# One kernel, one written order against another: retention attention and a gated channel mix on one core

## The chip, the cores and the metric

The kernel runs on one core of one Trainium2 chip. The time is device microseconds (us) from the core's first to its last instruction as the run reports it; three runs of the kernel before took 430.01, 433.79 and 429.88 us, median 430.01 us. Engines are called as the profile calls them: PE multiplies matrices, PEld is its weight load, DVE is the vector engine, ACT the scalar engine, POOL the GpSimd engine, SP issues the loads. Each engine works through its own instructions in the order in which they are written and stops at an instruction whose wait is not met.

## The reference

The inputs are q, k, v of shape (4, 8, 768, 64) (batch, heads, positions, head size), a decay `lam` per head, and for the second part `mu_k`, `mu_r` (512), `w_k` (512 x 1024), `w_v` (1024 x 512), `w_r` (512 x 512), all float32.

```python
# retention, per block of 64 positions
intra = ((qb @ kb.T) * Dmask) @ vb
inter = (qb * lam_pow) @ kv_state
out[block] = intra + inter
kv_state = lam_block * kv_state + (kb * rev_pow).T @ vb
# channel mix on x = the heads side by side, 512 wide
xk = mu_k * x + (1 - mu_k) * x_prev
xr = mu_r * x + (1 - mu_r) * x_prev
k = maximum(xk @ w_k, 0)
return sigmoid(xr @ w_r) * ((k * k) @ w_v)
```

`x_prev` is x moved by one position; `Dmask[i, j]` is `lam ** (i - j)` for i >= j and zero otherwise.

## The kernel before

The 768 positions are cut into six stages of 128 positions (n = 0 to 5), a stage of all four batches at once, 512 columns. The eight heads are four pairs (hp = 0 to 3). The whole program is one list of steps, the string `ORDER`; a step is a letter and two digits, and it is written out in the order of that string. So `ORDER` sets the order of each engine's instructions and of the loads on SP's queue. Every recorded instruction has line 30 of the file, so the trace is read by tile names.

The steps of a stage n and pair hp, with the tiles that the trace shows:

- `L`, `N`: SP loads of keys (`in<-kk`, 512 KB) and of queries and values (`in<-qv`, two of 256 KB); in stage 0 one load `L` (`in<-qvk`, 1 MB). Two buffers, `in0` and `in1`, are used by turns (hp % 2). `M`: POOL clears two blocks of the buffer (`MEMSET in`), which waits for the last reader of what lay there, the step `B` of the pair that used the buffer before.
- `A`: PE, scores into `sc`. `a`: DVE, times the decay table into `mv`. `q`: DVE, decayed queries into `mv`. `k`: ACT, decayed keys.
- `U`: PE, sums into `u` (one buffer). `u`: ACT copies the state into `in`, DVE updates the state `st`, ACT copies again. `w`: a second DVE update of `st`, which frees `u`.
- `B`: PE, values into `xp` (one buffer), from `in` and `mv`.
- `e`/`E`: ACT scales `xp` into `ts`, POOL copies one column (`ts<-lastw`, `lastw<-ts`). `f`/`F`: DVE mixes; in stage 0 the result is the fp32 tile `x`. `y`/`x`: ACT and DVE split the mix into a high part `xh` and a low part `xl` (`e`, `f`, `y` serve the input of k, `E`, `F`, `x` that of r).
- `R`/`Q`: PE, one pair's part of the receptance product, for batches 0-1 and 2-3, into four `rp` banks. `s`: ACT, sigmoid into `rt`.
- `K` (f = 0 to 7): PE, one eighth of the product with `w_k`, into a `kp` bank. `h`: ACT and DVE square it into `kf`. `p`: ACT and DVE split two eighths into `k` high and low; its DVE part writes `k<-kf,k`.
- `V` (i = 0 to 7): PE, batch i // 2, half i % 2 of the product with `w_v`, into a `vp` bank. `o`: DVE multiplies by `rt`, ACT issues the output transfer. For the last batch of the last stage V56 and V57 hold the multiplication and the transfer themselves, and `o53` does nothing.

`rp`, `kp` and `vp` share four PSUM banks. Products are taken in three fp32r passes (high by high, high by low, low by high), except in stage 0, where `R` and `K` run once in fp32, with the plain weights.

The weights arrive as 8-byte numbers and are turned into fp32 on the chip: `S` loads a slice (`wst`), `c` takes the magnitude on ACT and its maximum on POOL (on DVE for the first two slices of w_r; tile `wu`, one buffer), `C` puts the bits together in three DVE instructions (`wu`, `wst`, and `wr`, `wk` or again `wst`), `D` splits the slice on ACT and DVE into high and low (`hiv`, `lov` for w_v). `T` builds the decay tables on PE, `Z` runs matrix products of zeros.

Of the kernel before, what the change touches and what calls it, by code (L numbers as in the profile page):

```python
# [480 lines left out]


ORDER = """
Sr0 cr0 Cr0 Z10 T0 L00 Sr1 Z1 A00 k00 U00 a00 Z2 B00 cr1 L01 u00 Cr1 Sr2 k01 A01 a01 E00 U01 cr2 L02 u01 e00 T1 B01
Sr3 E01 L03 T2 F00 k02 Cr2 A02 f00 R00 e01 cr3 a02 U02 B02 M10 k03 u02 F01 f01 A03 Cr3 U03 Sk0 e02 R01 E02 a03 ck0 N10
L10 L11 Q00 f02 F02 R02 u03 Sk1 k10 q10 B03 N11 M11 Ck0 U10 E03 A10 Sk2 F03 Q01 R03 Q02 L12 e03 f03 ck1 u10 a10 B10
Sk3 N12 w10 Sv0 Sv1 M12 k11 U11 A11 s00 Ck1 Q03 s01 q11 E10 e10 ck2 k12 f10 u11 s02 K00 h00 a11 F10 A12 B11 M13 w11
L13 E11 Ck2 e11 a12 ck3 U12 K01 u12 f11 N13 K02 k13 s03 F11 Ck3 K03 w12 x10 cv0 A13 q12 B12 h01 h02 p00 h03 E12 N20
Sv2 Cv0 cv1 a13 L20 Dv0 U13 K04 u13 K05 Cv1 q13 K06 h04 p01 Dv1 K07 Sv3 M20 cv2 w13 A20 k20 U20 V00 h05 y10 L21 Cv2
k21 F12 e12 f12 V02 B13 h06 cv3 Dv2 M21 u20 Cv3 p02 N21 w20 h07 Dv3 p03 y11 x11 Dr0 V04 V06 q20 Dr1 U21 A21 V01 E13  # L490
V03 e13 V05 V07 o00 o01 a20 F13 f13 Dk0 B20 o02 o03 L22 y13 x12 R10 Q10 R11 Q11 R12 Q12 N22 u21 a21 x13 y12 Dk1 R13
Q13 L23 s10 q22 K10 s11 M22 E20 q21 K11 e20 s12 s13 w21 f20 F20 k22 U22 h10 A22 x20 Dk2 B21 K12 M23 a22 Dk3 K13 K14
h11 e21 N23 E21 F21 K15 h12 K16 p10 f21 h13 k23 u22 w22 B22 h14 U23 x21 A23 K17 p11 h15 E22 F22 u23 w23 V10 h16 y20
L30 p12 V12 a23 k30 V14 y21 e22 f22 M30 q23 h17 x22 L31 N30 A30 U30 p13 k31 B23 L32 V16 E23 V11 e23 a30 F23 u30 q30
N31 w30 V13 f23 M31 U31 y22 o10 B30 e30 u31 o11 A31 y23 k32 V15 o12 V17 R20 o13 E30 N32 q32 f30 x23 Q20 R21 Q21 R22
Q22 R23 L33 k33 Q23 q31 a31 M32 s20 w31 F30 s21 x30 B31 E31 e31 U32 F31 u32 w32 A32 a32 f31 M33 K20 s22 h20 L40 N33
K21 s23 B32 E32 F32 A33 x32 U33 h21 K22 u33 N40 q33 h22 L41 K23 h23 p20 k41 p21 K24 K25 h24 K26 K27 a33 h25 V20 k40
h26 p22 h27 y30 p23 w33 e32 f32 x31 V22 y31 V21 M40 B33 U40 A40 L42 M41 q40 e33 E33 f33 V24 u40 F33 N41 a40 w40 y32
V23 y33 B40 A41 o20 E40 U41 a41 F40 u41 V26 e40 L43 V25 V27 q41 x33 k42 o21 w41 o22 M42 f40 N42 A42 o23 B41 N43 U42
M43 L50 E41 a42 k43 u42 R30 F41 q42 w42 Q30 R31 Q31 R32 Q32 e41 R33 f41 Q33 x40 B42 s30 s31 U43 x41 A43 a43 E42 F42  # L500
q43 s32 s33 u43 w43 K30 N50 q50 x42 h30 K31 K32 h31 p30 K33 K34 h32 h33 p31 K35 h34 K36 h35 K37 L51 V30 h36 y40 e42
k50 y41 V32 V34 f42 h37 p33 p32 U50 B43 E43 A50 u50 V31 V33 y42 e43 N51 k51 F43 o30 f43 a50 q51 V35 V36 A51 U51 o31
B50 e50 a51 f50 o32 V37 E50 o33 u51 R40 Q40 F50 R41 Q41 B51 R42 Q42 x50 L52 k52 L53 x43 E51 F51 R43 y43 Q43 s40 N52
U52 N53 u52 q52 A53 s41 a53 s42 A52 K40 h40 q53 K41 h41 a52 s43 k53 K42 K43 h42 p40 K44 K45 K46 h43 h44 x51 p41 h45
e51 h46 f51 p42 K47 B52 h47 U53 y50 u53 p43 y51 V40 V42 e52 V41 E52 f52 V43 V44 F52 o40 y52 V46 V45 V47 B53 o41 o42
o43 x52 e53 f53 y53 R50 Q50 R51 Q51 R52 Q52 E53 F53 x53 R53 Q53 s50 s51 K50 K51 s52 h50 s53 h51 K52 h52 K53 h53 p51
p50 K54 h54 K55 h55 K56 K57 h56 h57 p53 V50 V52 V54 p52 V51 V53 o50 o51 V56 V55 V57 o52 o53
"""


# [51 lines left out]
```

## Time and profile before

| | |
|---|---|
| runs | 429.88, 430.01, 433.79 us, median 430.01 |
| profiled execution | span 430.3 us (no other time of it is given) |
| busy: PE, PEld | 419.5 us (98%), 328.9 us (76%) |
| busy: DVE, ACT, POOL | 264.0 us (61%), 204.9 us (48%), 71.0 us (16%) |
| chain that ended last | PE 81%, DVE 7%, DMA 6%, ACT 2%, POOL 1%, issue 1% |
| read from HBM, written | 35.83 MB, 6.29 MB |

A line of the timeline has the start, the duration, the engine, the operation with output and inputs, the count, and in brackets the idle time before it with what ended that. PE is busy in 98% of the span; the stretches in which it stands are read from its timeline.

### The profile page before, as it was taken

The page shows a single profiled execution, that of the slowest core. Times are in us where ns is not written, and L with a number is a line of the kernel's source. Part 1 is how long each engine was busy: PE and PEld are TensorE (multiplying, and loading weights), DVE is VectorE, ACT ScalarE, POOL GpSimd, SP SyncE. Part 2 cuts the span into 40 slices and gives each one's busy share as a digit, 9 for nine tenths or more (in the row PEclk, how much of TensorE's full clock was granted, in tenths as well). Part 3 has the DMA queues.
Part 4 walks back from the last instruction along what each step waited for, and adds up shares of the span by engine and source line. Part 5 has one row for each costly group of instructions (what it writes and reads, how often), then busy time and mean ns, then how long its engine had stood idle before and what let it go on. Part 6 is the DMA issues. An engine that isn't in the chain of part 4 may idle for free.

```text
span 430.3 us, 7314 instructions
## 1 busy us (share of the span) xinstructions
PE 419.5 (98%) x2935; PEld 328.9 (76%) x2935; DVE 264.0 (61%) x402; ACT 204.9 (48%) x357; POOL 71.0 (16%) x142
## 2 busy tenths in 40 slices
PE   7998899999999999999999999999999999999996
PEld 4665545668888888888888888888878888888885
DVE  5886999979867674746667646555437561414411
ACT  3645686586677643344644434454244460224300
POOL 4366554331102011110020200000000000000000
PEclk9999999999999999999999999999999999999999
DMA  7889918131403213515004523004520001100001
GB/s 295 304 308 330 300 48 277 66 97 50 146 3 99 87 46 107 153 58 140 0 2 131 187 78 99 0 0 123 161 62 0 2 1 50 50 2 0 0 30 69
DMA packets 12306, 42.60 MB, mean 99 GB/s; under 512 B 1776, under 2 KB 2160, under 8 KB 10736
## 3 DMA queue, kind: packets, MB, share of 16 engines
q1 hardware_dynamic: 8672, 35.84, 26.5%
q10 hardware_dynamic: 3600, 6.29, 4.0%
q8 instruction: 23, 0.38, 0.4%
q14 instruction: 11, 0.09, 0.1%
HBM read 35.83 MB, written 6.29 MB: 98 GB/s over the span
## 4 chain that ended last, share of the span: by engine, by line
PE 81%; DVE 7%; DMA 6%; ACT 2%; POOL 1%; issue 1%; SPq 0%; DVEq 0%; ACTq 0%
PE vp L30 29%; PE kp L30 26%; PE rp L30 13%; PE xp L30 5%; PE sc L30 4%; DMA wst<-w_k 4%; PE u L30 3%; DMA in<-qv 2%; DVE wst L30 2%; DVE mv L30 1%; DVE lov L30 1%; PE table L30 1%; ACT wu L30 1%; DVE wu L30 1%; POOL wu L30 1%
## 5 line engine op out<-in xcount | busy, mean ns | idle before, releaser
L30 PE MATMUL vp<-hiv,k 128*128 128x512 f32 (+1 forms) x400 | 122.8, 384 | 1.0 <-ACT kf L30 1.0
L30 PEld LDWEIGHTS vp<-hiv,k 128*128 128x128 f32 x400 | 74.1, 188 | 16.9 <-ACT kf L30 1.4
L30 PE MATMUL vp<-lov,k 128*128 128x512 f32 (+1 forms) x200 | 76.2, 381 | 0.0
L30 PE MATMUL kp<-xh,hik 128*128 128x512 f32 x160 | 62.9, 393 | 0.0
L30 PE MATMUL kp<-xl,hik 128*128 128x512 f32 x160 | 62.3, 389 | 0.0
L30 PE MATMUL kp<-xh,lok 128*128 128x512 f32 x160 | 62.3, 389 | 0.0
L30 ACT ACTIVATE ts<-xp,omu 128x512 f32<-128x512 f32 x48 | 31.8, 684 | 62.5 <-PE xp L30 44.2
L30 DVE TENSOR_TENSOR kf<-kp,kf 128x512 f32<-128x512 f32 x40 | 27.4, 688 | 37.2 <-ACT kf L30 37.1
L30 ACT ACTIVATE kf<-kp 128x512 f32<-128x512 f32 x48 | 28.4, 594 | 37.6 <-PE kp L30 37.2
L30 ACT COPY in<-st 64x256 f32<-64x256 f32 x80 | 32.3, 404 | 22.1 <-DVE st L30 17.8
L30 PEld LDWEIGHTS vp<-lov,k 128*128 128x128 f32 x200 | 37.6, 188 | 6.9
L30 DVE TENSOR_TENSOR mv<-sc,Dt 64x512 f32<-64x512 f32 (+1 forms) x48 | 32.6, 686 | 12.3 <-PE sc L30 11.9
L30 DVE TENSOR_TENSOR xl<-ts,xh 128x512 fp32r<-128x512 f32 x40 | 27.7, 703 | 19.3 <-ACT xh L30 19.2
L30 DVE SCALAR_TENSOR_TENSOR ts<-xp,smalls,ts 128x512 f32<-128x512 f32 x40 | 29.6, 747 | 15.8 <-ACT ts L30 15.6
L30 DVE TENSOR_TENSOR mv<-in,LP 64x256 f32<-64x256 f32 x80 | 34.5, 431 | 3.2 <-DMA in<-qv 1.6
L30 DVE TENSOR_TENSOR k<-kf,k 128x1024 fp32r<-128x1024 f32 x24 | 29.1, 1223 | 10.7 <-ACT k L30 10.7
L30 DVE TENSOR_TENSOR rt<-vp,rt 128x512 f32<-128x512 f32 (+1 forms) x25 | 16.4, 665 | 31.5 <-PE vp L30 31.2
L30 PEld LDWEIGHTS kp<-xh,hik 128*128 128x128 f32 x160 | 30.0, 188 | 7.0 <-issue 0.9
L30 PEld LDWEIGHTS kp<-xh,lok 128*128 128x128 f32 x160 | 30.0, 188 | 6.3
L30 PEld LDWEIGHTS kp<-xl,hik 128*128 128x128 f32 x160 | 30.0, 188 | 6.0
L30 ACT CAST xh<-ts 128x512 fp32r<-128x512 f32 x40 | 24.1, 616 | 21.7 <-DVE rt L30 18.2
L30 DVE SCALAR_TENSOR_TENSOR st<-st,LC,u 128x256 f32<-128x256 f32 x36 | 17.2, 478 | 24.8 <-ACT in L30 20.0
(70 smaller groups left out, 586.3 us busy)
## 6 DMA issues: line engine op xcount, KB each, us to landing
in<-qv SPq DMA_DIRECT2D x40, 256.0 KB, 4.5
in<-kk SPq DMA_DIRECT2D x20, 512.0 KB, 4.6
out<-rt ACTq DMA_DIRECT2D x23, 256.0 KB, 2.0
in<-qvk SPq DMA_DIRECT2D x4, 1024.0 KB, 6.3
wst<-w_k SPq DMA_DIRECT2D x4, 1024.0 KB, 9.2
wst<-w_v SPq DMA_DIRECT2D x4, 1024.0 KB, 9.7
wst<-w_r SPq DMA_DIRECT2D x4, 512.0 KB, 7.1
out<-rt ACTq DMA_DIRECT2D x2, 128.0 KB, 1.7
```

The costliest lines, as they stand in the source:

```text
L30: return lambda *args, **kw: self.tc.keep_in_program_order(op(*args, **kw))
```

## The change

`ORDER` is written anew: the same steps, in another order, and four more. Every step of the string before is there once, and `M50`, `M51`, `M52` and `M53`, which the string before did not have, clear the buffers ahead of stage 5 as well: eight more `MEMSET` of 64 x 512 on POOL. Every `M` now stands right behind the `B` that last reads the buffer. No line outside the string changes.

```diff
 ORDER = """
-Sr0 cr0 Cr0 Z10 T0 L00 Sr1 Z1 A00 k00 U00 a00 Z2 B00 cr1 L01 u00 Cr1 Sr2 k01 A01 a01 E00 U01 cr2 L02 u01 e00 T1 B01
-Sr3 E01 L03 T2 F00 k02 Cr2 A02 f00 R00 e01 cr3 a02 U02 B02 M10 k03 u02 F01 f01 A03 Cr3 U03 Sk0 e02 R01 E02 a03 ck0 N10
-L10 L11 Q00 f02 F02 R02 u03 Sk1 k10 q10 B03 N11 M11 Ck0 U10 E03 A10 Sk2 F03 Q01 R03 Q02 L12 e03 f03 ck1 u10 a10 B10
...
+Sr0 L00 cr0 Z10 T0 Z1 A00 Sr1 k00 T2 L01 U00 Cr0 a00 Z2 B00 cr1 Sr2 A01 E00 u00 Cr1 a01 e00 L02 k01 F00 cr2 T1 U01 B01
+f00 E01 u01 F01 k02 R00 A02 Sr3 e01 R01 U02 L03 Cr2 cr3 a02 B02 M10 Sk0 N10 k03 f01 e02 E02 u02 Cr3 L10 F02 Sk1 A03
+Q00 R02 a03 f02 q10 ck0 k10 Q01 U03 B03 M11 u03 E03 e03 Ck0 L11 N11 U10 F03 f03 o53 ck1 Sk2 A10 u10 a10 Sk3 Q02 Q03
+w10 R03 B10 M12 k11 Ck1 s00 q11 U11 s01 ck2 N12 e10 E10 u11 A11 L13 Ck2 f10 L12 s03 K02 s02 ck3 k13 K00 a11 k12 K01
+F10 w11 Ck3 q12 Sv0 h00 Sv1 Sv3 U12 h02 x10 B11 M13 cv0 A12 e11 a12 h01 Cv0 K03 E11 p00 F11 h03 cv1 K04 u12 K05 Sv2
+f11 Cv1 L20 K06 B12 M20 k20 w12 Dv0 N13 cv2 Dv1 U13 Cv2 h04 A13 h05 p01 p02 L21 cv3 K07 k21 V04 y10 x11 Cv3 h06 E12
...
```

Three places at which the instructions stand otherwise now. The first is PE at the end of the opening, where the first product with w_k begins. Before, B10 (`xp_474`), U11, A11 and the last receptance part are followed by K00 (`kp_558`, four rows) and then by A12 (`sc_569`):

```order
L30 MATMUL xp_474<-mv_405,in0_104 64x64 x16
L30 MATMUL u_504<-in1_105 64x128 x8
L30 MATMUL sc_513<-in1_105 64x128 x8
L30 MATMUL rp_392<-wr1_296,x32_7_95 128x512
L30 MATMUL rp_394<-wr1_296,x32_7_95 128x512
L30 MATMUL kp_558<-x32_0_88,wk0_425 128x512
L30 MATMUL kp_558<-x32_1_89,wk0_425 128x512
L30 MATMUL kp_558<-x32_2_90,wk1_526 128x512
L30 MATMUL kp_558<-x32_3_91,wk1_526 128x512
L30 MATMUL sc_569<-in0_104 64x128 x8
L30 MATMUL xp_578<-mv_532,in1_105 64x64 x16
L30 MATMUL u_617<-in0_104 64x128 x8
```

Now, from B10 (`xp_478`) on:

```order
L30 MATMUL xp_478<-mv_389,in0_104 64x64 x16
L30 MATMUL u_510<-in1_105 64x128 x8
L30 MATMUL sc_539<-in1_105 64x128 x8
L30 MATMUL kp_557<-x32_0_88,wk0_432 128x512
L30 MATMUL kp_557<-x32_1_89,wk0_432 128x512
L30 MATMUL kp_557<-x32_2_90,wk1_501 128x512
L30 MATMUL kp_557<-x32_3_91,wk1_501 128x512
L30 MATMUL kp_569<-x32_0_88,wk0_432 128x512
L30 MATMUL kp_569<-x32_1_89,wk0_432 128x512
L30 MATMUL kp_569<-x32_2_90,wk1_501 128x512
L30 MATMUL kp_569<-x32_3_91,wk1_501 128x512
L30 MATMUL kp_578<-x32_0_88,wk0_432 128x512
```

The receptance part has gone ahead of B10, three products with w_k (K02, K00, K01) stand in a row, and U12, B11 and A12 follow only behind the third.

The second place is the conversion of w_v, on POOL and on DVE. POOL before, from the maximum of the last w_k slice (`wu_614`) over those of the four w_v slices (`wu_662`, `wu_716`, `wu_780`, `wu_867`):

```order
L30 TENSOR_SCALAR wu_614<-wu_614 128x1024
L30 TENSOR_SCALAR wu_662<-wu_662 128x1024
L30 COPY ts_705<-lastw_113 128x4
L30 COPY lastw_113<-ts_705 128x4
L30 TENSOR_SCALAR wu_716<-wu_716 128x1024
L30 MEMSET in0_104 64x512 x2
L30 TENSOR_SCALAR wu_780<-wu_780 128x1024
L30 COPY ts_829<-lastw_113 128x4
L30 COPY lastw_113<-ts_829 128x4
L30 TENSOR_SCALAR wu_867<-wu_867 128x1024
```

POOL now, the same maxima being `wu_564` and `wu_637`, `wu_675`, `wu_732`, `wu_771`:

```order
L30 TENSOR_SCALAR wu_564<-wu_564 128x1024
L30 MEMSET in1_105 64x512 x2
L30 TENSOR_SCALAR wu_637<-wu_637 128x1024
L30 COPY ts_649<-lastw_113 128x4
L30 COPY lastw_113<-ts_649 128x4
L30 COPY ts_665<-lastw_113 128x4
L30 COPY lastw_113<-ts_665 128x4
L30 TENSOR_SCALAR wu_675<-wu_675 128x1024
L30 MEMSET in0_104 64x512 x2
L30 TENSOR_SCALAR wu_732<-wu_732 128x1024
L30 TENSOR_SCALAR wu_771<-wu_771 128x1024
```

A clear (`in1`, step M13) has come ahead of the first of the four. The clear of `in0` (M20) stands ahead of the third in both, but the step whose end it waits for, B12, has moved on PE from behind K03 to behind K06. DVE before, around the bits of the second slice (`wu_716`, `wst_498`) and the low part of `k` for eighths 2 and 3 (`k2_1_765`):

```order
L30 TENSOR_SCALAR wu_716<-wu_716 128x1024
L30 SCALAR_TENSOR_TENSOR wst_498<-wst_498,wu_716 128x1024
L30 SCALAR_TENSOR_TENSOR wst_498<-wst_498 128x1024
L30 TENSOR_TENSOR mv_719<-in1_105,LP_111 64x4x64 x4
L30 TENSOR_TENSOR k2_1_765<-kf_697,k2_1_765 128x2x512
L30 TENSOR_TENSOR lov1_85<-wst_498,hiv1_768 128x1024
```

DVE now, the low part of `k` being `k2_1_764` and the bits of the third slice `wu_732`, `wst_693`:

```order
L30 TENSOR_TENSOR lov0_84<-wst_594,hiv0_727 128x1024
L30 TENSOR_TENSOR lov1_85<-wst_599,hiv1_735 128x1024
L30 TENSOR_SCALAR wu_732<-wu_732 128x1024
L30 SCALAR_TENSOR_TENSOR wst_693<-wst_693,wu_732 128x1024
L30 SCALAR_TENSOR_TENSOR wst_693<-wst_693 128x1024
L30 TENSOR_TENSOR k2_1_764<-kf_612,k2_1_764 128x2x512
L30 TENSOR_TENSOR k2_2_767<-kf_750,k2_2_767 128x2x512
```

The low part of `k` stood behind the bits of the second slice and now stands behind those of the third.

The third place is the end of DVE's program. Before, the last stage's outputs are multiplied in the order o50, o51, V56, V57, o52:

```order
L30 TENSOR_TENSOR rt_3335<-vp_3473,rt_3335 128x512
L30 TENSOR_TENSOR rt_3337<-vp_3486,rt_3337 128x512
L30 TENSOR_TENSOR rt_3370<-vp_3542,rt_3370 128x256
L30 TENSOR_TENSOR rt_3370<-vp_3581,rt_3370 128x256
L30 TENSOR_TENSOR rt_3365<-vp_3499,rt_3365 128x512
```

Now o50, V56, o51, o52, V57:

```order
L30 TENSOR_TENSOR rt_3337<-vp_3476,rt_3337 128x512
L30 TENSOR_TENSOR rt_3378<-vp_3560,rt_3378 128x256
L30 TENSOR_TENSOR rt_3360<-vp_3521,rt_3360 128x512
L30 TENSOR_TENSOR rt_3358<-vp_3494,rt_3358 128x512
L30 TENSOR_TENSOR rt_3378<-vp_3591,rt_3378 128x256
```

The multiplication of PE's very last product, which had one more behind it, is now the last itself.

More of the change, by code (lines that the diff above doesn't have):

```diff
@@ L483 @@
 ORDER = """
-Sr0 cr0 Cr0 Z10 T0 L00 Sr1 Z1 A00 k00 U00 a00 Z2 B00 cr1 L01 u00 Cr1 Sr2 k01 A01 a01 E00 U01 cr2 L02 u01 e00 T1 B01
-Sr3 E01 L03 T2 F00 k02 Cr2 A02 f00 R00 e01 cr3 a02 U02 B02 M10 k03 u02 F01 f01 A03 Cr3 U03 Sk0 e02 R01 E02 a03 ck0 N10
-L10 L11 Q00 f02 F02 R02 u03 Sk1 k10 q10 B03 N11 M11 Ck0 U10 E03 A10 Sk2 F03 Q01 R03 Q02 L12 e03 f03 ck1 u10 a10 B10
-Sk3 N12 w10 Sv0 Sv1 M12 k11 U11 A11 s00 Ck1 Q03 s01 q11 E10 e10 ck2 k12 f10 u11 s02 K00 h00 a11 F10 A12 B11 M13 w11
-L13 E11 Ck2 e11 a12 ck3 U12 K01 u12 f11 N13 K02 k13 s03 F11 Ck3 K03 w12 x10 cv0 A13 q12 B12 h01 h02 p00 h03 E12 N20
@@ L489 @@
[L489 to L507, printed above, removed]
+Sr0 L00 cr0 Z10 T0 Z1 A00 Sr1 k00 T2 L01 U00 Cr0 a00 Z2 B00 cr1 Sr2 A01 E00 u00 Cr1 a01 e00 L02 k01 F00 cr2 T1 U01 B01
@@ new lines @@
+N20 Dv2 h07 V06 e12 Dv3 p03 Dk0 V00 f12 V02 a13 V05 V07 u13 V03 F12 V01 w13 Dr0 o02 U20 q13 B13 M21 Dr1 o03 o01 E13
+A20 o00 R10 R11 F13 Q10 y11 x12 x13 Q11 R12 L22 u20 Q12 R13 e13 q20 w20 N21 Dk1 a20 Q13 f13 s10 y12 A21 U21 s11 B20
+M22 y13 u21 e20 K10 K12 q21 s12 a21 E20 s13 K11 F20 h10 Dk2 k22 K13 f20 w21 Dk3 h12 N22 B21 M23 h11 q22 E21 U22 h13
+A22 e21 K16 p10 K15 f21 L30 K17 F21 L23 K14 k30 p11 h16 u22 a22 V16 h14 h17 B22 M30 N23 w22 A23 h15 k23 y20 U23 V12
+V10 L31 y21 x20 p13 a23 E22 N30 e22 V14 p12 u23 w23 V13 k31 A30 q23 f22 F22 q30 B23 M31 x22 x21 U30 u30 L32 a30 e23
@@ new lines @@
+f23 N31 V17 E23 V11 F23 V15 y22 o13 w30 o11 R20 B30 M32 o10 A31 o12 U31 E30 R21 R22 x23 N32 y23 e30 K20 k32 u31 R23
+K22 q31 F30 w31 f30 h20 U32 a31 A32 q32 s21 B31 M33 s20 Q20 x30 e31 Q21 h22 L40 Q22 K21 Q23 N33 E31 a32 K23 f31 k40
+u32 s22 L33 K24 k33 h21 s23 F31 w32 K25 p20 A33 U33 B32 M40 h23 K26 h24 a33 u33 q33 h25 L41 p21 K27 y30 k41 h26 E32
+V24 N40 x31 V22 V20 h27 V26 A40 p23 e32 q40 F32 y31 w33 f32 p22 x32 B33 M41 E33 U40 V27 e33 u40 V25 V23 N41 f33 w40
+a40 q41 y32 y33 F33 o22 U41 A41 x33 B40 M42 o21 V21 e40 R30 R31 f40 E40 R32 u41 o20 o23 L42 L43 R33 F40 K31 K30 s30
@@ new lines @@
+K32 h30 N42 s31 k42 a41 k43 w41 K33 h31 A42 q42 h32 B41 M43 p30 U42 E41 L50 F41 K34 h33 K35 h34 Q30 Q31 a42 e41 N43
+Q32 K36 Q33 u42 h35 x40 p32 K37 p31 f41 w42 U43 q43 h36 B42 M50 s32 y40 A43 a43 E42 h37 F42 e42 N50 s33 k50 y41 p33
+V34 f42 u43 y42 V32 V36 V30 A50 w43 B43 M51 L51 U50 k51 V33 e43 q50 u50 N51 V35 V31 x42 x41 E43 a50 o32 F43 o31 V37
+R40 o30 f43 y43 R41 B50 M52 o33 x43 U51 q51 A51 R42 N52 a51 E50 L52 e50 R43 f50 K40 K42 F50 L53 u51 k52 h40 B51 M53
+k53 s40 e51 A52 s41 U52 K41 K46 h41 N53 h42 p40 q52 Q40 Q41 K47 Q42 Q43 h46 E51 q53 u52 x50 s42 f51 s43 a52 K43 K45
@@ L508 @@
+A53 U53 h47 F51 h43 B52 u53 K44 p41 y50 h44 E52 V40 e52 h45 a53 F52 V42 V46 p42 p43 V47 f52 o43 y51 V41 x51 V44 B53
+E53 V43 o40 V45 F53 e53 x52 f53 o41 R50 o42 x53 R51 R52 R53 Q50 y53 Q51 y52 Q52 s50 Q53 K53 s52 s51 K52 h52 s53 K56
+h53 h56 K57 K50 p51 h57 p53 K51 h50 K54 h51 K55 p50 V50 h54 h55 V54 p52 V55 V52 V51 o50 V53 V56 o51 o52 V57
 """
```

## The prediction

> **What bounds the kernel now.** I read the page first, then PE's timeline, then the chain of waits, then the timelines of POOL and DVE at the places that the new order touches, and the landing times of single loads. The page:
>
> ```profile
> span 430.3 us, 7314 instructions
> PE 419.5 (98%) x2935; PEld 328.9 (76%) x2935; DVE 264.0 (61%) x402; ACT 204.9 (48%) x357; POOL 71.0 (16%) x142
> PEclk9999999999999999999999999999999999999999
> ```
>
> PE is busy for 419.5 of 430.3 us, at full clock in every slice. A new order removes no product, so all that it can win or lose is PE's standing time, 10.8 us. PE's timeline says where that lies (the bracket is the idle time before the row):
>
> ```profile
> 17.26 1.13 PE L30 MATMUL table<-lone 128*128 128x512 f32 x2
> 18.90 1.16 PE L30 MATMUL sc<-in 64*128 64x128 f32 x16 [0.51 <-DMA in<-qvk]
> 39.99 1.41 PE L30 MATMUL xp<-mv,in 128*64 128x64 f32 x32 [1.35 <-DVE mv L30]
> 45.12 3.60 PE L30 MATMUL kp<-x,wk 128*128 128x512 f32 x8
> 50.30 1.09 PE L30 MATMUL sc<-in 128*64 128x128 f32 x16 [1.59 <-DMA in<-qv]
> 64.55 1.10 PE L30 MATMUL xp<-mv,in 128*64 128x64 f32 x32
> 93.04 0.50 PE L30 MATMUL vp<-hiv,k 128*128 128x512 f32 x1 [0.99 <-ACT kf L30]
> ```
>
> The chain of waits has PE's end and what follows it:
>
> ```profile
> 404.17 22.10 PE vp L30 x120
> 426.30 0.42 DVE rt L30
> 426.72 0.60 DVEq L558
> ```
>
> From 93.04 us on PE never stands until 426.27. So the new order can win at four waits ahead of that: 0.51 (A02), 1.35 (B10), 1.59 (A12) and 0.99 us (V06). B10 hides a little more: it takes 1.41 us where B12 takes 1.10, so its second half waited 0.31. Together 4.75 us. Behind them lies the tail of 430.3 - 426.3 = 4.0 us. What PE stands before 17 us is counted at nothing: its start is the same decay tables and the same first products in both orders.
>
> **The change part by part.** *A02.* PE was free at 17.26 + 1.13 = 18.39 and waited for L02, which SP issues when B00 ends. The new order puts T2 (1.13) ahead of B00, which sends the load off so much later, but puts R00 ahead of A02:
>
> ```profile
> 19.99 1.98 PE L30 MATMUL rp<-wr,x 128*128 128x512 f32 x4
> 22.42 1.04 PE L30 MATMUL xp<-mv,in 128*64 128x128 f32 x16
> 23.39 1.16 PE L30 MATMUL sc<-in 64*128 64x128 f32 x16
> ```
>
> A part R of stage 0 takes 1.8 (5.42 us for three, below), so PE comes to A02 at 18.4 + 1.8 = 20.2 and the load is in at 18.9 + 1.1 = 20.0. The 0.51 goes, with 0.2 to spare.
>
> *R02.* Here a wait comes in. Its x needs B02, then ACT's scaling, and two column copies on POOL; POOL has M10 ahead of them, which starts when B02 ends:
>
> ```profile
> 23.59 1.95 POOL L30 MEMSET in<- 64x1024 f32 x2 [1.07 <-issue]
> 25.85 0.19 POOL L30 COPY ts<-lastw 128x4 f32<-128x4 f32 x1
> 33.82 0.75 DVE L30 SCALAR_TENSOR_TENSOR x<-xp,smalls,ts 128x512 f32<-128x512 f32 x1
> 33.22 5.42 PE L30 MATMUL rp<-wr,x 128*128 128x512 f32 x12
> ```
>
> From the clear's start to the end of the second copy: 25.85 + 0.19 - 23.59 = 2.45; with DVE's 0.75 and some hand-overs 3.4. Before, A03, U03, R01 and Q00 lay between B02 and R02; now only A03 and Q00, 1.1 + 1.8 = 2.9. New wait 0.5.
>
> *B10.* ACT stood for the second w_k slice, with U10's copies queued behind, and DVE stood behind those:
>
> ```profile
> 36.73 1.15 ACT L30 ACTIVATE wu<-wst 128x1024 f32<-128x1024 f32 x1 [1.44 <-DMA wst<-w_k]
> 27.38 9.33 DMA wst<-w_k
> ```
>
> In the new order SP issues Sk1 ahead of L11 and N11, right behind L10, and R03 (1.8) goes ahead of B10 together with Q02 and Q03, while R01 and U10 leave the stretch before it for an earlier place. I put the issue at 24 to 26 us; with 9.3 for the landing the slice is in at 33.5 to 35.6 instead of 36.7, and what follows on ACT and DVE comes 1.1 to 3.2 earlier. PE comes to B10 later: it was free at 39.99 - 1.35 = 38.64, and has now 0.51 less (A02), 0.5 more (R02) and Q03's 1.8 more ahead of it, 40.4. The 1.35 and the 0.31 both go. B10, U11 and A11 (1.0 each) then end at 43.4, where K02 starts.
>
> *A12.* The 1.59 is the load N12, which B10's end releases; it takes
>
> ```profile
> 41.43 8.73 DMA in<-qv
> 66.46 14.00 PE L30 MATMUL kp<-x,wk 128*128 128x512 f32 x32
> ```
>
> 8.7 us, and PE had only 50.30 - 1.59 - 41.43 = 7.3 of work in that time. Eight products of kp make one K00 to K07, so a K takes 14.00 / 4 = 3.5. Three of them now stand ahead of U12, B11 and A12, 10.5 us in place of one: the load is in about 5 us before PE asks. The 1.59 goes.
>
> *U12.* What comes next on PE behind those three needs k12 (ACT, on the load L12) and w11 (DVE, behind the conversion Ck2). U12 falls at 43.4 + 10.5 = 53.9. DVE's list to w11 ends at 52.4 to 53.4, if I lay its steps behind one another. L12 needs A11's end, 43.4; with the 8.7 of the load above it lands at 52.1, and k12's two scalings (about 0.9) end at 53.0. Both are less than 1.0 ahead of PE, so I take 0.3 (0 to 1.0).
>
> *V06.* Its 0.99 was the squaring h07 on ACT, which empties the bank that V06 writes and stood behind ACT's parts of the w_v conversion. In the new order V04 and V06 take banks that are emptied early, and h06 and h07 free those of V00 and V02; h07 ends by the list some 3.5 us behind the wait of V04 (next part), and the product on its bank starts some 7 us behind it. The 0.99 goes.
>
> *V04.* This is the largest new wait. POOL now has M20, which waits for B12, ahead of the maximum of the third w_v slice, and DVE has that slice's three bit instructions ahead of the low part of k for eighths 2 and 3, which V04 reads. B12 in turn has moved on PE to behind K06, a little ahead of K07 and V04. The rows of the pieces:
>
> ```profile
> 109.81 1.09 POOL L30 MEMSET in<- 64x512 f32 x2 [3.34 <-PE xp L30]
> 87.92 2.77 POOL L30 TENSOR_SCALAR wu<-wu 128x1024 f32<-128x1024 f32 x1 [1.93 <-ACT wu L30]
> 81.03 0.68 DVE L30 TENSOR_SCALAR wu<-wu 128x1024 int32<-128x1024 int32 x1
> 81.74 1.23 DVE L30 SCALAR_TENSOR_TENSOR wst<-wst,wu 128x1024 uint32<-128x1024 uint32 x1
> 83.00 1.23 DVE L30 SCALAR_TENSOR_TENSOR wst<-wst 128x1024 int32<-128x1024 int32 x1
> 94.26 1.22 DVE L30 TENSOR_TENSOR k<-kf,k 128x1024 fp32r<-128x1024 f32 x1
> 96.06 1.02 PE u L30 x16
> 97.08 0.87 PE sc L30 x16
> 93.04 3.01 PE vp L30 x12
> ```
>
> From B12's end: the second clear 0.55, the maximum 2.77, the bits 0.68 + 1.23 + 1.23, the low part 1.22, some 0.2 of hand-overs, together 7.9. PE has in that time U13 and A13 (0.9 each), K07 (3.5), the six products of V04 on eighths 0 and 1 (half of 3.01, 1.5) and two more (0.5): 7.2. That is 0.7. But POOL's next maximum, that of the fourth slice, starts at about the moment in which DVE starts the low part, and the two disturb each other where they met before:
>
> ```profile
> 77.50 3.27 POOL L30 TENSOR_SCALAR wu<-wu 128x1024 f32<-128x1024 f32 x1 [4.48 <-ACT wu L30]
> 78.05 2.06 DVE L30 TENSOR_TENSOR lov<-wst,hiv 128x1024 fp32r<-128x1024 f32 x1
> ```
>
> A subtraction of that size takes 1.22 alone and 2.06 here: 0.84 more, and the wait would be 1.5. I take 1.4, with ends of 0.6 and 2.0.
>
> The Trainium skill, page "SBUF — State Buffer", section "Who interferes with whom", says that a DVE instruction with two inputs in SBUF and a GpSimd operation that reads SBUF take one pair of ports as a lock, and that the later one stands for the whole length of the earlier. The trace does not agree in full: by that rule the subtraction that starts at 78.05 would have stood until the maximum's end at 80.77 and ended near 82.0, where its row ends at 80.11. What the rule would give here is a rival below.
>
> Behind V04 I went through each wait of both lists, stage by stage, with the durations of the rows: from stage 1 on every wait has 1.2 us or more of other PE work in front of it, and I count nothing for it. The eight new clears of stage 5 (8 x 0.55 = 4.4 us) run on POOL, which the page shows with no busy slice behind the middle of the span; they wait for nothing but B and are waited for by loads, whose landings lie a stage ahead of their readers. Nothing.
>
> *Fewer short runs.* In the row of 1.02 PE changes from long products to the short ones, in the next (0.87) it goes on with short ones: 0.15 for a change. The list of steps has 23 such changes instead of 25, 0.3.
>
> *The tail.* Before, DVE multiplied V57 and then, behind it, o52, whose 256 KB went out last. Now V57 is the last on DVE and its 128 KB the last out:
>
> ```profile
> out<-rt ACTq DMA_DIRECT2D x23, 256.0 KB, 2.0
> out<-rt ACTq DMA_DIRECT2D x2, 128.0 KB, 1.7
> ```
>
> The 0.60 of the second multiplication goes and 0.3 of the landing: 0.9 of 4.0.
>
> The sum on the profiled execution: 430.3 - 4.75 (four waits) - 0.9 (tail) - 0.3 (runs) + 0.5 (R02) + 0.3 (U12) + 1.4 (V04) = 426.5. The median of the runs is 430.0, 0.3 below the span, so 426.2.
>
> **The rivals.** *No new waits.* Each of R02, U12 and V04 is a difference of two sums of 3 to 10 us, and half a microsecond less on one side closes two of them. Against this speaks V04, whose 0.7 comes from rows alone. 430.3 - 4.75 - 1.2 = 424.4, as a median 424.1; with part of them 425.5.
>
> *The full lock.* If DVE's low part of k starts behind POOL's fourth maximum and stands for the whole 2.77 instead of losing 0.84, V04 waits up to 0.7 + 2.77 = 3.5 rather than 1.4; as the maximum has started somewhat earlier I take 1.9 more: 428.1. The pair of rows at 77.50 speaks against it. It is the rule of the Trainium skill's page told above.
>
> *A late w_k conversion.* Sk2's conversion, w11 and a11 stand in one list on DVE; if Sk2 lands 2 us later than I think, U12 waits 1 to 2 us more: 428. For it: several loads share the time from 27 to 50 us. Against it: the slice has been sent off earlier than before.
>
> *Slower: L12.* This load of keys is now issued at 43.4 us, where before another load of keys was issued, behind slices of w_v. Landings of these loads:
>
> ```profile
> in<-kk SPq DMA_DIRECT2D x1, 512.0 KB, 9.8
> in<-kk SPq DMA_DIRECT2D x1, 512.0 KB, 14.3
> ```
>
> The first was issued at 33.5, the second at 43.4 us. If L12 takes the 14.3 of the second it lands at 57.7, k12 ends at 58.6, and PE stands at U12 from 53.9 on: 4.7 us, 426.2 - 0.3 + 4.7 = 430.6, above the time before, and up to 433 if the loads behind it come late as well. It decides from a landing behind 53. Against it: the slow load stood behind w_v slices that had been issued earlier; L12 has none of them in front.
>
> *The change does nothing.* That the four waits only move: each would need a step late by as much as was won. The rows of PE under the change show other products in front of B10 and A12, so I give it little: 430.
>
> **How the numbers follow.** The forecast has a chance of 0.50, with 425.2 to 427.2 as its own range; no new waits 0.20 (424.1 to 425.5); the late conversion 0.11 (428); the full lock 0.08 (428.1); L12 0.07 (430.6 to 433); nothing 0.04 (430). The range reaches from 424.2 to 429.8, which leaves out the last two cases and the lowest end of the second. One per cent, about what a measurement of this kernel tells from no change, is 4.3 us: faster is below 425.7, slower above 434.3. Faster: the second case and about a quarter of the first (0.13), 0.33. Slower: the far end of the L12 case and what I have not thought of, 0.04. Same: the rest, 0.63.
>
> **What would show it.** In PE's timeline of the changed kernel: no bracket at A02, B10, A12 and V06; brackets of about 0.5 at R02's products near 28 us, up to 1 at U12 near 54, and 0.6 to 2 within V04 near 79 us, ended by DVE's `k`; the first `kp` row at 43 to 44 us; no bracket behind that; from PE's last product to the end of the span 3.1 instead of 4.0. A bracket of several us at U12 with the load `in<-kk` named would make it wrong upward; no bracket at V04 downward; brackets in the stages 1 to 5 would say that I misread the slack there.

## The result, and the profile after

Fifteen executions of the changed kernel have a median of 427.87 us (426.04 to 431.0), fifteen of the kernel before 431.5 us (429.79 to 433.79). The ratio is 0.9926, with an interval of 0.990 to 0.9952: the changed kernel is faster by 0.74%, or 3.2 us (2.1 to 4.3), which is less than the 1% that the prediction called telling apart.

The page of the changed kernel begins:

```profile
span 429.2 us, 7327 instructions
PE 421.7 (98%) x2935; PEld 331.1 (77%) x2935; DVE 261.5 (61%) x402; ACT 205.6 (48%) x357; POOL 75.6 (18%) x150
PEclk9999999999999999999999999999999999999999
```

This profiled execution took 431.0 us, the longest of the fifteen, for a span of 429.2. Every execution here gives both numbers, and the time is 1.8 above the span in all of them (426.04 beside 424.3 at the other end). So the execution whose profile the prediction worked from, span 430.3, is worth some 432.1 us: it was not 0.3 above the median, but longer than two of the three executions shown with it.

PE's timeline of the changed kernel holds these rows with a wait (in brackets) or at a place where the prediction spoke of one:

```profile
6.64 3.67 PE L30 MATMUL table<-rows 128*128 128x64 f32 x16 [0.21 <-DVE rows L30]
10.67 2.08 PE L30 MATMUL sc<-in 64*128 64x128 f32 x16
12.68 2.07 PE L30 MATMUL table<-lone 128*128 128x512 f32 x2
24.43 1.16 PE L30 MATMUL sc<-in 64*128 64x128 f32 x16 [1.04 <-DMA in<-qvk]
32.41 3.70 PE L30 MATMUL rp<-wr,x 128*128 128x512 f32 x8 [0.41 <-DVE x L30]
44.63 1.15 PE L30 MATMUL xp<-mv,in 128*64 128x64 f32 x32
47.46 10.57 PE L30 MATMUL kp<-x,wk 128*128 128x512 f32 x24
57.96 1.09 PE L30 MATMUL u<-in 128*64 128x128 f32 x16
84.07 0.74 PE L30 MATMUL vp<-hiv,k 128*128 128x512 f32 x2 [0.68 <-DVE k L30]
```

A02 (24.43) waits 1.04, R02 (32.41) 0.41, V04 (84.07) 0.68. B10 (44.63), the three products with w_k in a row (47.46) and U12 (57.96) wait for nothing, V06 neither, and nothing waits behind 84.07. The chain's end has no second multiplication any more, and from PE's end to the end of the span are 429.2 - 426.1 = 3.1 us, where there were 4.0:

```profile
404.03 22.08 PE vp L30 x120
426.14 0.42 DVE rt L30
```

The first three rows above are what the prediction had not looked at. The same products of the opening stand in the profile of before as

```profile
6.71 2.10 PE L30 MATMUL table<-rows 128*128 128x64 f32 x16 [0.28 <-DVE rows L30]
8.95 1.16 PE L30 MATMUL sc<-in 64*128 64x128 f32 x16
17.26 1.13 PE L30 MATMUL table<-lone 128*128 128x512 f32 x2
```

Until about 14.7 us PE ran at little more than half the pace in the changed kernel's profile, 1.57 + 0.92 + 0.94 and 0.25 of a product of zeros, 3.7 us in all, while the granted clock of the page is full in both. The trace's own record of that clock begins with its first change, at 6.94 us in the profile of before and at 14.79 us in this one; what lies ahead of it is printed as full. So the two profiles, one 1.1 us below the other, can't be set against each other as they are.

### The profile page after: what moved, and what is told of

Its sections match the earlier page's. It is cut to its first block, busy times and chain, and to the rows that moved or that the text cites. A ratio compares the mean times of both kernels' runs of the same rounds, so it can differ in the third digit from the quotient of the medians.

```text
span 429.2 us, 7327 instructions
## 1 busy us (share of the span) xinstructions
PE 421.7 (98%) x2935; PEld 331.1 (77%) x2935; DVE 261.5 (61%) x402; ACT 205.6 (48%) x357; POOL 75.6 (18%) x150
## 4 chain that ended last, share of the span: by engine, by line
PE 84%; DVE 6%; DMA 4%; POOL 3%; ACT 1%; issue 1%; SPq 0%; POOLq 0%; DVEq 0%; ACTq 0%
PE vp L30 31%; PE kp L30 26%; PE rp L30 14%; PE xp L30 4%; PE sc L30 4%; PE u L30 4%; POOL wu L30 2%; DMA wst<-w_k 2%; DVE wst L30 2%; DMA in<-qvk 2%; PE table L30 1%; DVE mv L30 1%; ACT wu L30 1%; DVE wu L30 1%; POOL in L30 1%
## 5 line engine op out<-in xcount | busy, mean ns | idle before, releaser
L30 POOL MEMSET in<- 64x512 f32 (+1 forms) x40 | 22.5, 562 | 180.5 <-PE xp L30 155.0
L30 DVE TENSOR_TENSOR xl<-ts,xh 128x512 fp32r<-128x512 f32 x40 | 26.6, 689 | 23.6 <-ACT xh L30 23.3
L30 PE MATMUL rp<-hir,xh 128*128 128x512 f32 x80 | 31.6, 395 | 0.0
```

The source lines that it names most:

```text
L30: return lambda *args, **kw: self.tc.keep_in_program_order(op(*args, **kw))
```

## The experiments

Each kernel below was timed against the kernel before, on three chips, where the kernel before has medians of 431.24, 432.06 and 430.94 us; so kernels are compared by their ratios, and their times only roughly. The intervals of the ratios are about 0.003 to either side, 1.3 us, so a single edit that is worth less than that is read from its profile.

### The opening

Two kernels change only the number of products of zeros ahead of the decay tables.

```diff
-Sr0 L00 cr0 Z10 T0 Z1 A00 ...
+Sr0 L00 cr0 Z4 T0 Z1 A00 ...
```

> The changed kernel with 4 products of zeros ahead of the decay tables instead of 10. The profile of the changed kernel has its 16 table products at 3.67 us where the kernel before has them at 2.10, and its executions lie between 426.0 and 431.0. Theory A: that spread is the moment at which PE's pace rises in the opening, and the products of zeros bring it about. With 4 of them (1.8 us) PE stands some 2.9 us ahead of the tables, the rise comes late in every execution, the table takes about 3.7, and the lowest of the executions is no longer near 426 but at 428.5 or above, with a smaller spread. Rival B: the spread comes from the landing of loads. Then the tables start at 6.6 as before, their pace has nothing to do with the zeros, and lowest and median stay where they are (426 and 428).

Measured: ratio 0.9963 (0.9936 to 0.999), median 430.45, executions from 428.59 to 432.56.

```diff
-Sr0 L00 cr0 Z10 T0 Z1 A00 ...
+Sr0 L00 cr0 Z16 T0 Z1 A00 ...
```

> The changed kernel with 16 products of zeros ahead of the tables instead of 10. Theory A (PE's pace rises at different moments of the opening): the rise falls within the zeros in nearly all executions; each zero takes 0.445 us before it and about 0.22 behind it, so the tables start at 7.7 to 9.1 instead of 6.6 and take 2.1; the highest execution falls from 431 to about 429, the lowest rises from 426.0 to about 427, the spread shrinks to 2 to 3 us, the median stays within 0.7 of 427.9. Rival B (loads make the spread): every execution is later by about 2.5, or by less where a load is waited for afterwards, and the spread stays at 5.

Measured: ratio 0.9905 (0.9872 to 0.9939), median 427.89, executions from 426.7 to 428.59. PE's timeline of the kernel with 4, and then of that with 16:

```profile
1.98 1.89 PE L30 MATMUL idle<-zeros 128*128 128x512 bf16 x4 [1.98 <-DVE zeros L30]
6.67 3.68 PE L30 MATMUL table<-rows 128*128 128x64 f32 x16 [2.80 <-DVE rows L30]
```

```profile
1.98 5.69 PE L30 MATMUL idle<-zeros 128*128 128x512 bf16 x16 [1.98 <-DVE zeros L30]
7.51 1.89 PE L30 MATMUL table<-rows 128*128 128x64 f32 x16
```

With 4 the tables are slow, and the lowest execution lies 2.5 above that of the changed kernel. With 16 the zeros themselves become fast under way (16 at 0.445 would be 7.1, they took 5.7), the tables are fast, and six executions spread over 1.9 us, where fifteen of the changed kernel spread over 5.0. Theory A foretold both; only the smaller spread with 4 did not come (4.0 in twelve). The spread by itself shows little, since two kernels below with 10 products of zeros also spread over 1.9 in six; the theory rests on the rows and on the lowest time with 4. With 10, which both orders have, it differs from one execution to the next: slow tables in the profile of the changed kernel, fast ones in several below. The Trainium skill, page "TensorE: Matmul & The Clock Gate", section "Part 1: The HAM clock gate", has this as a rule: PE's array runs at half its clock until it has been busy through a window of some 3.4 us, and since the window is not tied to the kernel's start, the same kernel rises at different products. The rows here agree in the factor (0.445 against about 0.23 for a product of zeros, one taking 0.38 and two 0.61) and in that it varies, and in the kernel with the tail alone the record of the clock changes at 5.28, 8.69 and 12.10 us, 3.41 apart; its advice that the loss is below 1% of a kernel holds too (3.7 of 429), but here that is more than the whole change.

### The new waits of the changed kernel

A02: T2 moved to where PE waits.

```diff
-... A00 Sr1 k00 T2 L01 U00 ... U01 B01 f00 E01 u01 F01 k02 R00 A02 ...
+... A00 Sr1 k00 L01 U00 ... U01 B01 f00 E01 u01 F01 k02 R00 T2 A02 ...
```

> The changed kernel with the table step T2 moved back from ahead of U00 to directly ahead of A02. In the profile of the changed kernel PE waits 1.04 us at A02 for the load L02, which B00's end sends off; T2's two products take 2.07 there. Theory A: B00 ends 1.1 to 2.1 earlier, so the load does too, and T2 now lies in the stretch in which PE waited: the wait goes, and the time falls by about 1.0 against the changed kernel (the ratio to the kernel before falls from 0.9926 to about 0.990). Rival: the loads behind it share the same queues, L02 lands as late as before, and what is won at A02 is waited for at R02 or A03: no change.

Measured: ratio 0.9936 (0.9903 to 0.9968), median 429.79: no gain. The profile, with slow tables again (3.67):

```profile
22.54 1.10 PE L30 MATMUL table<-lone 128*128 128x512 f32 x2 [0.42 <-DVE lone L30]
23.56 1.16 PE L30 MATMUL sc<-in 64*128 64x128 f32 x16
31.55 3.70 PE L30 MATMUL rp<-wr,x 128*128 128x512 f32 x8 [0.42 <-DVE x L30]
```

A02 (23.56) waits no more, but T2 itself now waits for its operand on DVE. Both this and the rival's reason (a wait further on) are small beside the opening, and the times don't tell them apart.

R02: Q01 ahead of it.

```diff
-Q00 R02 a03 f02 q10 ck0 k10 Q01 U03 B03 ...
+Q00 Q01 R02 a03 f02 q10 ck0 k10 U03 B03 ...
```

> The changed kernel with the receptance part Q01 moved from behind R02 to ahead of it. R02 waits 0.41 us for DVE's x in the profile of the changed kernel; Q01 is 1.8 us of work that needs nothing new. Theory A: the wait goes and nothing comes in its place: 0.4 less, a ratio of about 0.9917. Rival: U03 and B03, which Q01 stood in front of, then wait by as much: no change (0.9926).

Measured: ratio 0.987 (0.9836 to 0.9904), median 426.28 (425.4 to 427.34). In its profile (span 423.8, tables 2.37) neither A02 nor R02 waits; behind the opening PE waits once, as the view of the waits has it (time in all, times, longest):

```profile
PE vp L30 <- DVE k L30: 0.7, 1, 0.7
PE table L30 <- DVE rows L30: 0.2, 1, 0.2
```

V04: the clear M20 moved out of the way of the third maximum.

```diff
-... K06 B12 M20 k20 w12 Dv0 N13 cv2 ... L21 cv3 K07 ...
+... K06 B12 k20 w12 Dv0 N13 cv2 ... L21 cv3 M20 K07 ...
```

> The changed kernel with the clear M20 moved from ahead of the maximum of the third w_v slice to behind that of the fourth. V04 waits 0.68 us for DVE's low part of k in the changed kernel. The prediction's chain (B12, clear, maximum, bits, low part of k) says that without the two clears the maximum starts 1.1 us earlier, the wait goes and the time falls by 0.7 (ratio from 0.9926 to about 0.991). Rival: the maximum then waits for ACT's magnitude anyway, or the next step in V04 (the low part of w_v's slice, the next w_v slice) is late instead: no change.

Measured: ratio 0.985 (0.9812 to 0.9887), median 425.76 (425.4 to 427.28); its interval lies wholly below that of the changed kernel. All waits of PE behind the first tables in its profile (span 423.6, tables 2.00):

```profile
PE rp L30 <- DVE x L30: 0.4, 1, 0.4
PE sc L30 <- DMA in<-qvk: 0.3, 1, 0.3
```

V04's wait is gone and nothing has come in its place. In the five profiles of the new order that keep M20 ahead of the third maximum V04 waits 0.67 to 0.70 us, in the three that move it not at all: that the wait hangs on this clear is shown. Here the opening was fast as well, and part of the 0.0076 between the two ratios may be that.

The two edits last shown, Q01 and M20, together:

> The changed kernel with Q01 ahead of R02 and M20 behind the fourth maximum. The profile of Q01 alone shows only the wait of 0.69 at V04 left, beside the opening. If the two add up: no wait of PE behind the opening at all, and 0.7 less than Q01 alone (median 425.6, lowest 424.7, ratio 0.985). Rival: the opening decides, and the 0.7 is lost in its spread or in a new wait behind V04: 426.3.

Measured: ratio 0.9883 (0.9837 to 0.9929), median 427.32 (425.43 to 430.82): not better than either alone. Its profile has a fast opening (2.00) and neither R02's nor V04's wait, but others:

```profile
25.79 1.16 PE L30 MATMUL sc<-in 64*128 64x128 f32 x16 [1.24 <-DMA in<-qvk]
34.08 1.09 PE L30 MATMUL u<-in 128*64 128x128 f32 x16 [0.29 <-POOL wu L30]
38.85 3.70 PE L30 MATMUL rp<-wr,x 128*128 128x512 f32 x8 [0.89 <-DVE x L30]
```

The first is the load L03, which was sent off at 18.0 us and landed 7.6 later; in the profile with Q01 alone it was sent off at 18.2 and took 5.3. So beside the opening the landings of the loads differ from one execution to the next, by more than the waits in question.

The three edits of the opening, R02 and V04 at once, with half of the zeros cleared (only that half is read) so that PE starts earlier:

```diff
-    vector.memset(zeros, 0.0)
+    vector.memset(zeros[:, 0:512], 0.0)
...
-Sr0 L00 cr0 Z10 T0 ...
+Sr0 L00 cr0 Z14 T0 ...
-Q00 R02 a03 f02 q10 ck0 k10 Q01 U03 ...
+Q00 Q01 R02 a03 f02 q10 ck0 k10 U03 ...
-... B12 M20 k20 ... cv3 K07 ...
+... B12 k20 ... cv3 M20 K07 ...
```

> The changed kernel with three edits: Q01 ahead of R02, M20 behind the fourth maximum, and an opening that PE's pace can't miss: only the half of the zeros that is read is cleared, so PE starts at 1.5 instead of 2.0, and 14 products of zeros stand ahead of the tables instead of 10. Theory (the pace of the opening makes most of the spread, V04 and R02 hold the last waits): lowest about 425.0 as in the single edits, highest not above 428.5, median 425.7, ratio about 0.986; the profile shows the tables at 2.0 to 2.4. Rival (what is left of the spread comes from the landings of L02 and L03, which differ by 2 us between profiles): spread stays at 5 and the median at 427.

Measured: ratio 0.9889 (0.9853 to 0.9925), median 426.47 (425.32 to 428.06). The spread is 2.7 in six executions where the changed kernel had 5.0 in fifteen, the highest 2.9 below that of the changed kernel, the tables take 2.00, as the theory had it; the median is 0.8 above its number. What PE waits for behind the opening:

```profile
24.72 1.16 PE L30 MATMUL sc<-in 64*128 64x128 f32 x16 [0.56 <-DMA in<-qvk]
33.07 1.09 PE L30 MATMUL u<-in 128*64 128x128 f32 x16 [0.35 <-issue]
```

Again a load (L03) stands there. This kernel and the three with one or two of its edits lie between 0.985 and 0.9889, and their intervals do not separate them from one another.

### Parts of the change, put into the kernel before

The clears alone: every `M` of the kernel before directly behind its `B`, and M50 to M53. Two of the places:

```diff
-... q12 B12 h01 h02 p00 h03 E12 N20 ... K07 Sv3 M20 cv2 ...
+... q12 B12 M20 h01 h02 p00 h03 E12 N20 ... K07 Sv3 cv2 ...
-... V02 B13 h06 cv3 Dv2 M21 u20 ...
+... V02 B13 M21 h06 cv3 Dv2 u20 ...
```

> The kernel before with nothing but the clears moved: every M directly behind the B that last reads its buffer, and the four new clears of stage 5. The prediction gives the clears no gain of their own: the four waits of PE in the kernel before (A02, B10, A12, V06) hang on loads and conversions, not on a clear. So 0, with at most 1 us lost where a clear that waits for B stands ahead of a maximum on POOL. Rival: the clears are what makes the gain, since loads and sums of the next pair wait for them: 3 us less, as in the changed kernel.

Measured: ratio 1.0 (0.9973 to 1.0028). The clears by themselves make no gain. The cost that the prediction had seen for a clear ahead of a maximum is in its profile, in rows of POOL, DVE and PE:

```profile
89.85 1.10 POOL L30 MEMSET in<- 64x512 f32 x2 [2.77 <-PE xp L30]
90.91 2.92 POOL L30 TENSOR_SCALAR wu<-wu 128x1024 f32<-128x1024 f32 x1
93.87 0.69 DVE L30 TENSOR_SCALAR wu<-wu 128x1024 int32<-128x1024 int32 x1 [2.27 <-POOL wu L30]
98.14 0.47 DVE L30 SCALAR_TENSOR_TENSOR st<-st,LC,u 128x256 f32<-128x256 f32 x1
98.71 1.09 PE L30 MATMUL u<-in 128*64 128x128 f32 x16 [1.58 <-issue]
```

The clear waits for B13, the maximum of the fourth slice stands behind it (90.91; in the profile of before it ran from 87.92, with PE 1.1 us ahead), DVE waits 2.27 for that, and with it the update of the state that frees `u`, which ends at 98.61: PE stands 1.58 until 98.71, though the view names no releaser. That is more than the 1 us that was allowed for.

The tail alone:

```diff
-p50 K54 h54 K55 h55 K56 K57 h56 h57 p53 V50 V52 V54 p52 V51 V53 o50 o51 V56 V55 V57 o52 o53
+p50 K54 h54 K55 h55 K56 K57 h56 h57 p53 V50 V52 V54 p52 V51 V53 o50 o51 V56 V55 o52 V57 o53
```

> The kernel before with o52 moved ahead of V57, and nothing else. The prediction's tail term: the 0.60 of a second multiplication behind PE's last product and 0.3 of the last transfer go, 0.9 less (430.5 in place of 431.4), and the profile shows 3.1 from PE's end to the end of the span instead of 4.0. Rival: the last transfer's landing ends the span whatever stands before it: no change.

Measured: ratio 0.9958 (0.9927 to 0.9988), 0.5 to 3.1 us less. The chain's end, in a span of 430.4:

```profile
405.20 22.10 PE vp L30 x120
427.32 0.42 DVE rt L30
```

From PE's end, 427.3, to the end of the span are 3.1. The 0.9 is shown.

B10: the second w_k slice sent off earlier.

```diff
-ck0 N10 L10 L11 Q00 f02 F02 R02 u03 Sk1 k10 ...
+ck0 N10 Sk1 L10 L11 Q00 f02 F02 R02 u03 k10 ...
```

> The kernel before with one load moved on SP's queue: the second w_k slice (Sk1) ahead of L10 and L11, which it stood behind. The prediction's reason for B10: the slice lands about 2 us earlier, ACT and DVE come through, and B10's 1.35 goes in the executions that have it: 0.7 to 1.6 less (ratio 0.9965 to 0.998). Rival: what B10 wins is waited for at A12, whose load N12 is sent off by B10's end but shares the queues with w_k and w_v: no change.

Measured: ratio 1.0027 (0.9994 to 1.006), no gain. B10 doesn't wait in its profile (nor in those of the other kernels with the order before, below), but a step ahead of it does:

```profile
33.39 1.33 PE L30 MATMUL u<-in 128*64 128x128 f32 x15 [1.97 <-ACT in L30]
```

That is U10, whose decayed keys hang on the load L10, which now stands behind the slice. The rival had the wait come back, at A12; it came back at U10. The changed order has Sk1 behind L10 and ahead of L11, and there U10 waits for nothing.

A12: one more product ahead of it.

```diff
-... K00 h00 a11 F10 A12 B11 M13 w11 L13 E11 Ck2 e11 a12 ck3 U12 K01 u12 ...
+... K00 h00 a11 F10 K01 A12 B11 M13 w11 L13 E11 Ck2 e11 a12 ck3 U12 u12 ...
```

> The kernel before with K01 moved from behind U12 to ahead of A12. The prediction's reason for A12: PE gets 3.5 us more of work while N12 lands, so the 1.59 goes in the executions that have it: 0.7 to 1.6 less (ratio 0.9965 to 0.998). Rival: A12, B11 and U12 come 3.5 later, and the steps that hang on them (a12, u12, M13, N13) hold up a later A13 or B12 by as much: no change or slower by up to 1.

Measured: ratio 1.0052 (1.0022 to 1.0082), slower by 2.2 us. Its profile:

```profile
62.84 0.30 PE L30 MATMUL xp<-mv,in 128*64 128x64 f32 x2 [1.77 <-DVE mv L30]
63.29 1.88 PE L30 MATMUL xp<-mv,in 128*64 128x64 f32 x29 [0.15 <-DVE mv L30]
```

A12 doesn't wait, and B12 does, for DVE, as its rival had it. But V06 now waits 0.2 instead of some 1.0, and B11 not at all, so these waits alone don't make 2.2. Behind B12's wait PE's granted clock falls. The view by stretches (stretch, its length, PE busy and count, granted clock, share of DMA, GB/s):

```profile
63.80:67.10 3.30, 3.27 (x37) 0.50 0.30 93
```

Half the clock for the 3.41 us of its record, 63.78 to 67.19, is 1.7 us of PE's work. Nine of the twelve executions have a mean clock of 0.997 or less, where 2 of the 29 executions of the kernel before beside them have one. So the move brings a wait, and in most executions a fall of the clock with it.

The two moves that the prediction credited with B10 and A12 gain nothing in the order before. They could gain little there, since only the profile of before has those waits. What in the new order keeps PE from standing a few steps further on was not tried by itself.

### The kernel before with a sure opening

```diff
-    vector.memset(zeros, 0.0)
+    vector.memset(zeros[:, 0:512], 0.0)
...
-Sr0 cr0 Cr0 Z10 T0 L00 ...
+Sr0 cr0 Cr0 Z14 T0 L00 ...
```

> The kernel before with the same opening of zeros (half the clear, 14 products), and its order kept otherwise. Profiles of the order before: with slow tables (3.7 us) B10 and A12 don't wait, with fast ones (2.1) they wait 1.35 and 1.59. Theory: its loads and conversions of w_k set the pace there, so a fast opening is given back at B10 and A12: median within 0.7 of 431.5, the profile shows fast tables and waits at B10 or A12. Rival: a fast opening is worth the same 3.7 in both orders: median near 430.0, its lowest below 429.0.

Measured: ratio 0.9971 (0.9951 to 0.9992), median 430.09 (429.54 to 431.78). The spread is 2.2 in twelve executions where 29 of the kernel before beside it spread over 4.4, and eleven of the twelve lie between 429.5 and 430.6, where 9 of the 29 do. Its waits behind the tables:

```profile
18.96 1.16 PE L30 MATMUL sc<-in 64*128 64x128 f32 x16 [0.73 <-DMA in<-qvk]
49.10 1.15 PE L30 MATMUL xp<-mv,in 128*64 128x64 f32 x32 [0.88 <-DVE ts L30]
91.14 0.50 PE L30 MATMUL vp<-hiv,k 128*128 128x512 f32 x1 [1.15 <-ACT kf L30]
```

The tables are fast (2.00) and neither B10 nor A12 waits, so the theory, that a fast opening is given back at these two, falls. The median goes with the rival, whose lowest below 429.0 did not come (429.54); B11's wait, the longest of its kind, may be where part of it is given back.

What differs from the profile of before is the loads. B10 there hangs on the second slice of w_k, which was sent off at 27.38 us and landed 9.3 later. Ahead of it SP's queue had stood for 1.8 us. The wait in the profile of before, then the sending and the landing of the same slice in the kernel with K01 moved, whose order and tables (2.00) are like those of before up to B10:

```profile
SPq L30 <- ACT st L30: 1.8, 1, 1.8
```

```profile
25.42 0.43 SPq L30 DMA_DIRECT2D wst<-w_k  x1
wst<-w_k SPq DMA_DIRECT2D x1, 1024.0 KB, 9.1
```

There the slice landed as slowly, was sent off 2.0 us earlier, and B10 waits for nothing. So against that kernel it is the late sending, not the landing, that makes B10's wait (with the sure opening the slice was sent off at 26.36 and landed in 6.9); why SP's queue stood is open, since the kernel with K01 moved issued the same load ahead of that step of ACT. A12 hangs on N12. The second of its two loads landed 8.7 us after it was sent off in the profile of before, and 7.1, 6.9, 6.3 and 7.0 in the kernels with the tail, the clears, the sure opening and K01 moved; PE's work beside it is the 7.3 us that the prediction counted.

## Why the prediction was right, and where it was not

The time, 427.87, lies in the range (424.2 to 429.8), the likeliest class (within 1%) is the one that came, and the drop that the sum gave, 430.3 to 426.5, is 3.8 us, inside the measured 2.1 to 4.3. But the forecast of 426.2 is 1.7 low, and that the drop comes out near is in good part luck: the gain at B10 and A12 was counted 2.3 to 2.7 us too high, that in PE's own work 1.6 too low, and the losses at V04 and U12 together 1.0 too high, which nearly cancel. Waits in the profiles of the order before:

| profile | tables | A02 | B10 | A12 | B11 | V06 |
|---|---|---|---|---|---|---|
| before | 2.10 | 0.51 | 1.35 | 1.59 | none | 0.99 |
| tail alone | 2.56 | 0.60 | none | none | 0.67 | 1.08 |
| clears alone | 3.68 | 0.49 | none | none | 0.51 | 0.99 |
| sure opening | 2.00 | 0.73 | none | none | 0.88 | 1.15 |

*The base.* "The median of the runs is 430.0, 0.3 below the span" is the step that failed first. A time is 1.8 above its span, so the sum, made against the profiled execution, belongs to one of 432.1, and its end, 426.5, to a time of 428.3. The median came to 427.87.

*B10 and A12, 3.25 of the 4.75.* They are waits of that one execution, in which the second slice of w_k was sent off late and N12 landed late (shown above). In the other profiles of this order they are absent and B11 waits 0.5 to 0.9 instead; what the prediction called hidden in B10's row, 0.31, is there 0.3 (tail alone, the row takes 1.41), 0.1 (sure opening, 1.25) and nothing. The new order does remove whatever stood there: none of its eight profiles has a wait at B10, A12 or B11. But the typical gain of that stretch is 0.5 to 1.0, not 3.25. The prediction also has R03 and Q02 going ahead of B10; both stood ahead of it before, and its sum rightly counts Q03 alone.

*V06.* Right: about 1.0 in every profile in the table, none in any of the new order.

*A02.* It was to go with 0.2 to spare. In the profiles of the new order with T2 in its new place it is 1.04 (the changed kernel), 0.28 (M20 moved) and none in the other five; three of these wait 0.45 to 1.24 at A03 for the next load instead. The margin is smaller than what a load's landing varies by.

*R02.* 0.5 foretold, 0.41 measured, and gone when Q01 was put ahead. *U12.* 0.3 foretold, none measured; L12 came in time, so the slower rival did not happen, nor the late conversion.

*V04.* 1.4 foretold, 0.68 measured, and the 0.7 that came from rows alone was the right half (its terms for PE add up to 7.3, not 7.2, which makes it 0.6); the other half, 0.84 for POOL's next maximum beside DVE's low part of k, is the mis-sized term. DVE's piece in the chain, its row in the timeline (with the low part for the next two eighths) and POOL's row:

```profile
82.88 1.15 DVE k L30
82.80 3.19 DVE L30 TENSOR_TENSOR k<-kf,k 128x1024 fp32r<-128x1024 f32 x2
82.91 3.73 POOL L30 TENSOR_SCALAR wu<-wu 128x1024 f32<-128x1024 f32 x1 [3.29 <-ACT wu L30]
```

The low part started just ahead of the maximum and was not slowed; the maximum took 3.73 instead of 2.77. So did the maximum of the second slice (68.51, 3.71), which began 0.14 behind a single low part of k (68.37, 1.22). The full lock of the rival did not cost PE anything, since DVE came first. By the Trainium skill's rule (page "SBUF — State Buffer", section "Who interferes with whom") the later of the two stands for the whole of the earlier, by which the maximum would have stood until the low part's end at 84.03, some 1.1 us; it took 0.96 longer, so this pair is near the rule. The second low part is not, like the pair in the prediction: it began behind the maximum, took some 2.0 and ended at 85.99, where by the rule it would have stood until the maximum's end at 86.64.

*Behind V04.* That PE waits for nothing behind V04 was right, in the changed kernel and in all its variants.

*The tail.* 0.9 foretold, 4.0 to 3.1 measured, and shown by itself.

*Fewer short runs, 0.3.* Too small, or there is more. From the pages of the kernel before with the sure opening, and of the kernel with all three edits, which has the same number of zeros:

```profile
PE 420.1 (98%) x2939; PEld 329.3 (77%) x2939; DVE 263.7 (62%) x402; ACT 205.4 (48%) x357; POOL 71.7 (17%) x142
```

```profile
PE 418.0 (99%) x2939; PEld 328.8 (78%) x2939; DVE 262.2 (62%) x402; ACT 205.5 (49%) x357; POOL 77.8 (18%) x150
```

PE is busy for 2.1 us less, of which 0.2 lies in the zeros (5.30 against 5.11). The term gave 0.3. In the chain of the changed kernel a change back from short to long products shows too, 2.94 against 2.72 for twelve products, 0.22 that I had not counted; with it two changes fewer make 0.7. Of the other 1.2, 0.5 lies in three rows of the opening that take longer in the first kernel without a bracket: U00 0.92 against 0.69, B00 1.22 against 1.09, B10 1.25 against 1.15. Where the remaining 0.7 comes from I have not found. The difference is not that of two executions: less the zeros and the first tables PE is busy for 412.8 to 413.0 us in the three profiles with fast tables and the order before (before, Sk1 earlier, sure opening), and for 410.8 to 411.2 in the five with fast tables and the new order.

So the account between those two kernels, spans 428.4 and 423.6: waits 0.73 + 0.88 + 1.15 against 0.56 + 0.35, 1.9 less (two of the new waits have been taken out of the second kernel, 1.1 together); the tail 0.9 less; PE's work 2.1 less, together 4.9 for 4.8 measured. Without those two edits some 3.7 are left, near the 3.2 of the result.

That the tail is worth 0.9, and that neither the clears nor the two single moves gain anything in the order before, while the whole order does, is shown. Which others of the many moves the gain in B10's and A12's stretch and in PE's work needs was not tried.

## What to carry to other kernels

Where a change is worth 1%, look at more than one profile: a wait that stands in one execution can be that execution's own late loads, and its removal is no gain in the others. Compare the first products of the two profiles before comparing anything else, since PE's pace there can differ by more than the change, and read the granted clock stretch by stretch behind every wait of PE of a microsecond or two: one wait of 1.8 us cost another 1.7 in clock here. A wait cured by moving one step tends to come back a few steps on, in the step whose operand stood behind the moved one; price the queue that it moves past.
